# Gate matmuls around the last scale's transpose, the next attention begun in the output stage, and a new order of the attention steps

## The chip, the cores and the metric

The kernel runs on one core of a Trainium2 chip (trn2). Its time is in device microseconds. TensorE multiplies matrices and writes to PSUM; VectorE, ScalarE and GpSimd do the rest (GpSimd does not touch PSUM here); SyncE (SP) issues most DMAs, GpSimd a few.

## The reference

Four batches of 576 tokens go through three blocks. The first is attention with 8 heads of width 64: scores q k^T / 8, plus a decay (the difference of running sums of log f), causal, softmax, times v. The second takes x (the heads side by side, 512 wide):

```
mixed = real(fft(fft(x, axis=1), axis=2))
u = x + mixed
un = (u - mean) / sqrt(var + 1e-6)
x2 = u + relu(un @ w_ch1) @ w_ch2          # 512 -> 2048 -> 512
```

The third is gated over tokens:

```
h = relu(x2 @ w_in); u, v = h[:512], h[512:]
v_n = (v - mean) / sqrt(var + 1e-6)
out = (u * (w_spatial @ v_n + b_spatial)) @ w_out
```

## The kernel before, in words

Values are split into two float16 parts (high and low), and each product is three matmuls (`PASSES`), so most of the time goes to matmuls with 128 x 128 weights.

For one batch the work has two halves. The *attention half* takes four head pairs. Each has a load of q and k into a buffer `a` (`attn_load`), a stack (`attn_stack`: transposes `pk` and `pq`, high and low parts back into `a`, then DMAs `S<-a` into the operands S1 and S2), five max groups (`attn_max`: matmuls `mxd`, `mxa`, `mxb`, `mxc`, reductions on VectorE, and the transposes `mxt` that bring the row maxima into S2), four score groups (`attn_scores`: `sc`, two exponentials, the low part by a subtraction on VectorE, or on GpSimd in batch 0 where `XPOOL` says so) and the product with v (`attn_pv`). v is loaded into `vraw`, reduced and scaled (`v_load`, `v_prep`). Then come `fold` (sums and differences that halve the transform), the token stage `dft1` (tile `yps`), the feature stage `dft2` (tile `eo`, sums added to X) and `norm_tile` (statistics, `un`, and the transposes `tr` into `unT` and `uT`).

The *matmul half* is `mlp1` and `mlp2`. `mlp1` takes three tiles of 192 tokens, for each eight pairs of `first` (`ph`) and `second` (`acc`). At the end of a tile, `acc` is added to `uT` (L927), its largest value `xmx` is reduced (L931), and `scale` turns it into a power of two: a transpose on TensorE (`p2ps`, L268), a short chain on VectorE, and the scaled tokens in `unT` (L938, L939). The scale of the third tile is kept as `state[b]["last"]` and called in `mlp2`. `mlp2` makes the gate half v in five token tiles (`vpart`, tile `pvv`, then its normalisation on ScalarE, VectorE and GpSimd), the u half (`upart`, tile `pu`), the spatial product (`vs`), its split into `gT` and `GT`, and the output (`po`, `ob`, DMA).

The two halves overlap: while TensorE does the matmul half of batch b, the attention half of batch b + 1 is dealt out between its pieces. `mlp1` and `mlp2` are generators that yield a nominal time after each piece (3.87, 2.6, 2.0, 1.7); `xlater` lists the attention steps with nominal times from the table `LATER`, and `run` issues at each yield all steps whose time has come:

```
while evs and (t1 is None or evs[0][0] <= t1):
    evs.pop(0)[1]()
```

So the order on TensorE is written out by hand (`MANUAL`). The lists of the other engines are made by a planner, which places an instruction when its own time model has it ready, by priority in the order of the program. Each engine then works its list in order. SP's list is by hand for batch 0's attention half (`START`), and by the planner after it.

Buffers tie the order too. `a` of one batch and `gu` of the other share one buffer (tag "a"), `vraw` and X share one (tag "X"), and `wps`, `xe`, `xo`, `vr`, `un`, `es`, `tt` and `ob` share three (tag "s2"). PSUM has two pieces for the attention half (`px`) and two of each of two kinds for the matmul half (`py`). Batch 0's attention half runs before the rest, beside the loading and splitting of the weights (`load_w`: GpSimd multiplies by the sign, L363, and subtracts, L366); what is left of the weights and `load_spatial` (transposes `wpps`, L388) is dealt out in batch 0's matmul half by `wsteps`.

Of the kernel before, what the change touches and what calls it, by code (L numbers as in the profile page):

```python
# [15 lines left out]
AF = mybir.ActivationFunctionType  # L16
# [34 lines left out]
QSTART = [0, 128, 256, 320, 448]  # L51
# [74 lines left out]
score1 score1 score1 score1 score1 max2 score1 score1 score1 max2 score1 score1 load3 max2 max2  # L126
max2 score1 w17 part0 score1 pv1 max2 pv1 max2 stack3 stack3 max2 w33 max2 max2 w32 score2
score2 score2 w3 score2 score2 score2 max3 score2 max3 score2 score2 max3 max3 score2 score2
max3 max3 score2 max3 max3 max3 max3 pv2 score3 score3 score3 score3 score3 score3 score3 score3
pv2 w0 w1 score3 score3 part1 score3 score3 part2 w2 pv3 w1 pv3 part3 fold0 fold0 fold2 fold1  # L130
fold1 w1 fold2 tok0 tok1 tok1 tok0 w1 w0 feat0 feat0 w0 w0 feat1 feat0 norm0 feat1 w0 feat2
feat1 w1 norm0 norm0 w2 w2 w3 norm1 norm1 w2 w3 norm0 w2 w4 w4 w4 w3 w3 w4 w5 w4 w5 feat2 w5 w5
w6 norm1 w6 w6 w8 w6 w7 w6 w5 w9 w8 w10 w8 w8 w8 w7 w7 w10 w7 w7 w10 w9 w10 w10 w12 w12 w12 w9
w9 w12 w12 w9 w11 w11 feat2 w11 w14 w14 w13 w11 w11 w13 w15 w13 w13 w13 w15 w14 w15 norm1 w15
w15 w14 w14
"""
# [3 lines left out]
def tile_kernel(  # L140
# [40 lines left out]
    o = 0  # L181
# [325 lines left out]
    def attn_max(b, hp):  # L507
# [459 lines left out]
    def mlp2(b):  # L967
# [27 lines left out]

        def vpart(i):
            n = 128 if i < 4 else 64
            rowscale(i)
            pv = yps("pvv", [128, DM])
            for kc in range(4):  # L1000
                for j, (a, e) in enumerate(PASSES):
                    T.matmul(  # L1002
                        pv[:n, :], xT[:, a, kc, 128 * i:128 * i + n], WI[:, e, kc, DM:2 * DM],
                        start=(kc == 0 and j == 0), stop=(kc == 3 and j == 2),
                    )
            vr = rp.tile([128, DM], F32, name="vr", tag="s2", bufs=NS2)
            A.activation(out=vr[:n, :], in_=pv[:n, :], func=AF.Relu)
# [108 lines left out]

    def xlater(b):

# [8 lines left out]

        L = LATER
# [114 lines left out]
```

## Time and profile before

| | us |
|---|---|
| median of 3 runs | 1000.13 (997.85 to 1002.47) |
| profiled execution | 997.69 |
| its span, first to last instruction | 995.9 |
| TensorE busy | 855.9 (86%) |
| VectorE / ScalarE / GpSimd busy | 596.6 / 397.9 / 270.5 |
| mean granted TensorE clock | 0.929 |

In the rows, PE is TensorE, PEld its weight loads, DVE VectorE, ACT ScalarE, POOL GpSimd and SP SyncE; SPq is SyncE's list of DMA issues. L512 is a line of the kernel. `mxd<-S` names the tile written and the one read. A bracket such as [7.23 <-DMA S<-a] is the time that the engine stood idle just before, and what ended that.

### The profile page before, as it was taken

To read this page: it belongs to the slowest core of one execution; us is meant where nothing else is said; L and a number is where in the kernel's file an instruction comes from. 1 tells how busy PE (TensorE), PEld (TensorE's weight loads), DVE (VectorE), ACT (ScalarE), POOL (GpSimd) and SP (SyncE) were. 2 spreads that over 40 slices of the span, in tenths; PEclk is the share of its full clock that TensorE was granted. 3 is DMA by queue.
4 is the path that set the end of the run, shared out by engine and by line. 5 is a ranking of instruction groups with operands and counts; after the bars stand their busy time and mean duration, and the time that the engine had idled before them with its cause. 6 is when DMAs were issued, how large, how long until landed. Compare 5 with 4: busy or idle time off the path is not lost.

```text
span 995.9 us, 22491 instructions
## 1 busy us (share of the span) xinstructions
PE 855.9 (86%) x9437; PEld 735.2 (74%) x9437; DVE 596.6 (60%) x1437; ACT 397.9 (40%) x697; POOL 270.5 (27%) x371
## 2 busy tenths in 40 slices
PE   3766335888999799699999799799999799999998
PEld 2655224787899568489999587589999486999884
DVE  4666789796754757365774775465674873122341
ACT  1846455767534333252334234144233334111132
POOL 4565887655500533000000440000000540000010
PEclk9886656898999899899999999899999999999999
DMA  7773316916210000722010001622100001000001
GB/s 152 211 213 100 115 64 195 218 48 171 86 35 18 13 7 2 173 61 48 17 38 2 1 2 49 137 61 62 33 7 2 1 2 43 2 2 1 2 1 53
DMA packets 75020, 60.89 MB, mean 61 GB/s; under 512 B 59869, under 2 KB 60263, under 8 KB 74791
## 3 DMA queue, kind: packets, MB, share of 16 engines
q1 hardware_dynamic: 74199, 58.13, 22.5%
q8 instruction: 74, 1.21, 0.5%
q0 software_dynamic: 720, 1.33, 0.5%
q14 instruction: 27, 0.22, 0.1%
HBM read 40.43 MB, written 4.83 MB: 45 GB/s over the span
## 4 chain that ended last, share of the span: by engine, by line
PE 55%; DVE 4%; DMA 2%; ACT 1%; SPq 0%; issue 0%; POOL 0%; ACTq 0%; DVEq 0%
PE ph L897 14%; PE acc L918 13%; PE vs L1051 6%; PE pu L989 4%; PE po L1069 4%; PE pvv L1002 4%; PE sc L618 1%; PE sc L622 1%; PE pv L685 1%; PE mxt L589 1%; PE tr L868 1%; PE yps L777 1%; DMA S<-a 1%; PE pv L687 1%; PE pv L686 1%; DMA vraw<-in_v_dram 1%
## 5 line engine op out<-in xcount | busy, mean ns | idle before, releaser
L897 PE MATMUL ph<-unT,W 128*128 128x192 f16 x2304 | 216.1, 253 | 4.9 <-DVE unT L712 3.6
L897 PEld LDWEIGHTS <-W 128*128 128x128 f16 x2304 | 199.8, 101 | 10.6 <-issue 4.2
L918 PE MATMUL acc<-hT,W 128*128 128x192 f16 x2304 | 205.7, 246 | 0.0
L918 PEld LDWEIGHTS <-W 128*128 128x128 f16 x2304 | 192.1, 98 | 0.2
L903 ACT ACTIVATE hT<-ph 128x384 f16<-128x384 f32 x96 | 46.9, 489 | 158.9 <-PE ph L897 157.1
L904 DVE SCALAR_TENSOR_TENSOR hT<-ph,hT 128x384 f16<-128x384 f32 x96 | 53.0, 552 | 84.7 <-ACT hT L903 84.7
L642 ACT ACTIVATE P<-sc 128x1024 f16<-128x1024 f32 (+1 forms) x64 | 53.9, 842 | 70.5 <-DVE sc L635 52.9
L656 DVE TENSOR_TENSOR P<-sc,P 128x1024 f16<-128x1024 f32 (+3 forms) x51 | 50.7, 994 | 31.8 <-ACT sc L654 30.7
L618 PE MATMUL sc<-S 128*128 128x256 f16 (+2 forms) x288 | 53.6, 248 | 11.4 <-DVE P L656 5.5
L687 PE MATMUL pv<-vh,P 128*128 128x65 f16 (+2 forms) x480 | 57.6, 200 | 4.6 <-DVE P L656 3.3
L975 POOL COPY tsc<-sc 128x2 f32<-128x2 f32 (+1 forms) x24 | 4.2, 195 | 209.9 <-DVE sc L947 209.5
L495 POOL COPY a<-a 128x2 f16<-128x2 f16 x32 | 5.8, 190 | 197.2 <-ACT a L492 143.9
L685 PE MATMUL pv<-vh,P 128*128 128x65 f16 (+2 forms) x480 | 58.4, 202 | 0.4 <-ACT sc L654 0.4
L1002 PE MATMUL pvv<-WI,unT 128*128 128x512 f16 (+1 forms) x240 | 58.5, 399 | 0.0
L686 PE MATMUL pv<-vh,P 128*128 128x64 f16 (+2 forms) x480 | 57.7, 200 | 0.0
L1051 PE MATMUL vs<-WP,vn 128*128 128x288 f16 x448 | 56.2, 286 | 0.0
L622 PE MATMUL sc<-S 128*128 128x256 f16 (+2 forms) x288 | 54.9, 248 | 0.0
L687 PEld LDWEIGHTS <-P 128*128 128x128 f16 (+2 forms) x480 | 48.7, 108 | 5.2 <-DVE P L656 3.6
L1051 PEld LDWEIGHTS <-vn 128*128 128x128 f16 x448 | 43.7, 98 | 10.9
L685 PEld LDWEIGHTS <-P 128*128 128x128 f16 (+2 forms) x480 | 48.0, 106 | 3.8 <-ACT sc L654 0.6
L363 POOL TENSOR_TENSOR WO<-WO,W 128x512 f32<-128x512 f32 x32 | 42.0, 1319 | 28.9 <-DVE WO L354 24.7
L989 PE MATMUL pu<-unT,WI 128*128 128x192 f16 x576 | 49.3, 246 | 0.0
(229 smaller groups left out, 1675.3 us busy)
## 6 DMA issues: line engine op xcount, KB each, us to landing
S<-a SPq DMA_DIRECT2D x96, 144.2 KB, 2.9
WI<-in_moe_w_ch_dram SPq DMA_DIRECT2D x16, 512.0 KB, 4.3
W<-in_moe_w_ch_dram SPq DMA_DIRECT2D x16, 512.0 KB, 4.3
a<-in_k_dram SPq DMA_DIRECT2D x32, 144.0 KB, 2.8
a<-in_q_dram SPq DMA_DIRECT2D x32, 144.0 KB, 4.7
vraw<-in_v_dram SPq DMA_DIRECT2D x16, 256.0 KB, 4.8
WP<-in_moe_w_in_dram SPq DMA_DIRECT2D x8, 512.0 KB, 4.3
out_dram<-ob SPq DMA_DIRECT2D x16, 256.0 KB, 2.2
```

Of the source, the lines that this page charges most:

```text
L618: T.matmul(ps[:, j, c0:c0 + w], S2[s][:, j, QN + 128 * kt:QN + 128 + 128 * kt], qh, start=i == 0, stop=False,)
L622: T.matmul(ps[:, j, c0:c0 + w], S1[s][:, j, 128 * kt:128 * kt + 128], q1, start=False, stop=last and b not in PEMASK,)
L642: A.activation(out=pt[:, 0], in_=src, func=AF.Exp, scale=1.0 / 2048.0)
L685: T.matmul(ps[:n, j, o0:o0 + 65], hi, vh[:kk, 0, kt, h, :], start=(i == 0), stop=False)
L686: T.matmul(ps[:n, j, o0:o0 + 64], hi, vh[:kk, 1, kt, h, 0:64], start=False, stop=False)
L687: T.matmul(ps[:n, j, o0:o0 + 65], lo, vh[:kk, 0, kt, h, :], start=False, stop=(i == len(jobs) - 1),)
L897: T.matmul(ph[:, c, :], W1[:, a, kc, 128 * ff:128 * ff + 128], unT[:, e, kc, tok(t)], start=(c == 0 and kc == 0 and i == 0), stop=(c == 1 ...
L904: V.scalar_tensor_tensor(out=hT[:, 1], in0=ph, scalar=0.0, in1=hT[:, 0], op0=ALU.max, op1=ALU.subtract)
L918: T.matmul(acc[t][d // 2][:, d % 2, :], W2[:, a, ff, 128 * d:128 * d + 128], hT[:, e, c, :], start=(ff == 0 and i == 0 and d % 2 == 0), st ...
L989: T.matmul(ph[:, c, :], WI[:, a, kc, 128 * ff:128 * ff + 128], xT[:, e, kc, tok], start=(c == 0 and kc == 0 and i == 0), stop=(c == 1 and ...
L1002: T.matmul(pv[:n, :], xT[:, a, kc, 128 * i:128 * i + n], WI[:, e, kc, DM:2 * DM], start=(kc == 0 and j == 0), stop=(kc == 3 and j == 2),)
L1051: T.matmul(ps, vn[:kk, a, s, 128 * c:128 * c + 128], WP[:kk, e, s, tok], start=i == 0, stop=i == len(jobs) - 1,)
```

## The change

- The gate stage: `vpart` is divided into `vmat` (matmuls) and `vnorm` (scale factors and normalisation). Two groups of gate matmuls now come before the transpose of the last scale, and the first normalisation, a u group, the second normalisation and the third gate group after it. Before, one gate group with its normalisation came first.
- Attention steps of batch b + 2 are put in the list before the matmul half of b begins instead of after it, so those with negative times are issued within the output stage of b. Times change in `LATER`, batch 1 has a table of its own (`SECOND`), and `V1` goes.
- `attn_max` no longer transposes column 576, a second copy of token 288 (one value a head), by a matmul of its own; VectorE copies it from column 288.
- `VSIGN`: the sign of weight tiles 0, 1 and 5 is put in by VectorE and not by ScalarE and a GpSimd multiplication. `XADDV`: in batch 0, the feature sums of token tile 0 are added on GpSimd. `XPOOL`: in batch 0, the low part of the second score group of the last head pair is made on GpSimd.
- `START` is broken into other lines; its words are the same.

```
-VSIGN = range(0, 0)
-LATER = {'per': 20.875, 'off': -10.0, 'v': (-8.0, 7.0, 9.5), 'load': (17.0, 20.0), 'max': (7.5, 9.5, 12.0, 16.0, 18.5), 'score': (24.5, 23.5, 26.5, 35.5), 'pv': 38.5, 'fold': (93.5, 94.61, 97.7), 'tok': (109.0, 112.27), 'feat': (113.5, 117.99, 119.21), 'norm': (127.0, 121.0, 122.5, 133.5, 126.0), 'out': (134.53, 135.55, 139.09, 142.58, 134.16)}
+VSIGN = (0, 1, 5)
+LATER = {'per': 21.047, 'off': -10.01, 'first': -10.02, 'v': (-8.38, 6.04, 10.17), 'load': (27.96, 17.77), 'max': (7.48, 9.42, 11.98, 15.89, 18.19), 'score': (24.13, 23.07, 26.13, 35.18), 'pv': 38.84, 'fold': (92.29, 93.4, 97.55), 'tok': (109.1, 115.66), 'feat': (118.95, 120.08, 120.91), 'norm': (130.1, 121.74, 128.73, 133.36, 129.96), 'out': (134.19, 138.29, 138.61, 142.1, 132.79)}
+MLP = [26 * 3.87 + 5 * 2.6 + 6 * 2.0 + 8 * 1.7 + n * 2.6 for n in (4, 5)]
-NORM2 = (0.1, 2.673, 2.948)
-V1 = (14.0, 15.5, 16.5)
+NORM2 = (0, 2.838, 3.101)
+SECOND = {'per': 20.875, 'off': -10.13, 'first': -9.5, 'v': (4.87, 15.39, 16.25), 'load': (18.8, 21.49), 'max': (7.5, 9.5, 12.0, 15.56, 18.5), 'score': (24.5, 22.76, 26.5, 35.5), 'pv': 38.16, 'fold': (97.35, 97.43, 100.52), 'tok': (104.42, 111.18), 'feat': (112.33, 117.99, 116.42), 'norm': (128.81, 125.43, 119.33, 134.84, 127.84), 'out': (135.15, 135.63, 139.17, 142.25, 134.24)}
-XADDV = (0, 4)
+XADDV = (4,)
-XPOOL = (3, 3, 4, 3)
+XPOOL = (3, 4, 4, 3)
...
-            jobs = [(t, QSTART[t], 0, QWIDE[t]) for t in range(5)] + [(2, S, 32, 1)]
-            for t, o, r, n in jobs:
+            for t, o in enumerate(QSTART):
+                n = QWIDE[t]
                 T.matmul(
-                    pm[96:128, j, o:o + n], mc[r:r + n, j, t, :], eyeh[r:r + n, r:r + n],
+                    pm[96:128, j, o:o + n], mc[:n, j, t, :], eyeh[:n, :n],
...
-        A.activation(out=S2[s][96:128, :, 0:S + 1], in_=pm[96:128, :, 0:S + 1], func=AF.Copy)
+        A.activation(out=S2[s][96:128, :, 0:S], in_=pm[96:128, :, 0:S], func=AF.Copy)
+        V.tensor_copy(S2[s][96:128, :, S:S + 1], pm[96:128, :, 288:289])
...
-        vpart(0)
+        vmat(0)
+        yield 2.6
+        vmat(1)
         yield 2.6
         state[b]["last"]()
-        vpart(1)
-        yield 2.6
-        vpart(2)
-        yield 2.6
+        vnorm(0)
         upart(0, 0)
         yield 2.0
-        vpart(3)
+        vnorm(1)
+        vmat(2)
+        vnorm(2)
         yield 2.6
-        vpart(4)
+        vmat(3)
+        vnorm(3)
+        yield 2.6
+        vmat(4)
+        vnorm(4)
         yield 2.6
...
-        at("v", *(L["v"] if b > 1 else V1))
+        at("v", *L["v"])
         for hp in range(NP):
-            t0 = L["off"] + L["per"] * hp
-            at(f"load{hp}", t0 - (L["load"][0] if hp == 0 else L["load"][1]))
+            t0 = L["off"] + L["per"] * hp if hp else L["first"]
+            at(f"load{hp}", max(t0 - L["load"][1], last + 0.1) if hp else t0 - L["load"][0])
+            last = t0
...
-        nxt = xlater(1)
+        nxt = xlater(1, {**LATER, **SECOND})
...
         for b in range(B):
-            base = now
+            total = MLP[b % 2]
+            if b + 2 < B:
+                nxt = nxt + [(t + total, f) for t, f in xlater(b + 2)]
+            now = 0.0
             for i, dt in enumerate(mlp(b)):
...
-                run(nxt, now - base)
-            total = now - base
-            if b + 2 < B:
-                more = [(t + total, f) for t, f in xlater(b + 2)]
-                nxt = sorted(nxt + more, key=lambda e: e[0])
+                run(nxt, now)
```

## Rows read from the trace of the kernel before

**Rows 1.** Busy time by stretch: PE, PEld, DVE, ACT, POOL (instructions), granted clock, DMA share, GB/s.
```profile
100.00:125.00 25.00, 8.55 (x60) 5.44 (x61) 19.04 (x44) 12.39 (x24) 21.89 (x19) 0.64 0.37 108
...
400.00:425.00 25.00, 16.57 (x111) 11.15 (x110) 10.17 (x26) 5.04 (x8) 0.37 (x2) 0.80 0.71 157
...
875.00:900.00 25.00, 25.00 (x305) 24.99 (x304) 7.25 (x17) 3.88 (x7) 0.30 (x2) 1.00 0.01 2
```

**Rows 2.** TensorE's waits, whole span: who waited for what: us in total, times, longest.
```profile
PE mxd L512 <- DMA S<-a: 26.0, 5, 7.4
...
PE eo L810 <- ACT yc L783: 3.9, 2, 3.7
```

**Rows 3.** Timeline of TensorE, boundary of batch 0 and 1: start, busy us, instruction, idle before.
```profile
410.03 0.66 PE L482 MATMUL pq<-cft,a 96*128 96x96 f32 x6
417.91 1.10 PE L512 MATMUL mxd<-S 126*128 126x128 f16 x4 [7.23 <-DMA S<-a]
...
420.87 0.93 PE L512 MATMUL mxb<-S 126*128 126x128 f16 x4 [1.11 <-DVE mcol L527]
421.59 3.52 PE L897 MATMUL ph<-unT,W 128*128 128x192 f16 x24
```

**Rows 4.** Timeline of VectorE in that wait.
```profile
410.26 2.29 DVE L428 TENSOR_REDUCE vmx<-vraw 128x1 f32<-128x2048 f32 x1 [6.35 <-DMA vraw<-in_v_dram]
```

**Rows 5.** TensorE's waits from 630 to 642 us, boundary of batch 1 and 2.
```profile
PE mxd L512 <- DMA S<-a: 5.3, 2, 5.1
PE mxb L512 <- DVE mcol L527: 1.1, 1, 1.1
```

**Rows 6.** Timeline of TensorE, end of the first stage, batch 1, then batch 3.
```profile
564.45 0.45 PE L268 MATMUL p2ps<-cft,xmx 128*128 128x128 f32 x1 [4.98 <-DVE xmx L931]
564.69 6.87 PE L1002 MATMUL pvv<-WI,unT 128*128 128x512 f16 x24
...
941.76 5.34 PE L1002 MATMUL pvv<-WI,unT 128*128 128x512 f16 x24
```

**Rows 7.** Timeline of TensorE and VectorE, end of the first stage of batch 0.
```profile
343.17 0.87 PE L388 MATMUL wpps<-cft,wps 128*128 128x128 f32 x3 [7.12 <-DMA wps<-in_moe_w_spatial_dram]
...
344.50 0.41 DVE L712 TENSOR_TENSOR xoh<-a,xoh 128x256 f16<-128x256 f32 x1
...
371.71 0.43 PE L799 MATMUL eo<-xeh,tab 128*65 128x1 f16 x9 [1.32 <-DVE tt L824]
```

**Rows 8.** The chain that ended last: start, us, what.
```profile
402.54 5.18 PE po L1069 x24
...
460.60 1.33 PE mxt L589 x12
```

**Rows 9.** Timeline of VectorE: the scaled tokens of batch 1's last tile.
```profile
570.79 0.99 DVE L939 SCALAR_TENSOR_TENSOR unT<-uT,sc,unT 128x768 f16<-128x768 f32 x1
```

**Rows 10.** Timeline of SP's DMA issues, both boundaries.
```profile
398.07 1.05 SPq L467 DMA_DIRECT2D a<-in_q_dram  x2
...
402.95 4.49 SPq L419 DMA_DIRECT2D vraw<-in_v_dram  x5
...
632.80 1.13 SPq L500 DMA_DIRECT2D S<-a  x2
```

**Rows 11.** Line 467, 612 to 635 us: the loads of q and k.
```profile
DMA to landing us min/median/max: 2.7/2.8/2.9
```

**Rows 12.** Busy time by stretch, columns as in rows 1.
```profile
556.70:572.00 15.30, 10.32 (x48) 4.68 (x46) 14.11 (x36) 5.10 (x11) 9.13 (x15) 0.89 0.00 0
388.90:392.10 3.20, 2.70 (x27) 2.44 (x26) 2.49 (x8) 1.89 (x5) 0.00 (x0) 1.00 0.00 0
```

**Rows 13.** Timeline of TensorE in batch 0: a wait of 2.18 us and what followed.
```profile
242.43 0.19 PE L618 MATMUL sc<-S 128*128 128x65 f16 x1 [2.18 <-DVE P L656]
...
243.11 3.66 PE L897 MATMUL ph<-unT,W 128*128 128x192 f16 x24
```

**Rows 14.** The page's costliest groups: count, busy us and mean ns, idle before.
```profile
L363 POOL TENSOR_TENSOR WO<-WO,W 128x512 f32<-128x512 f32 x32 | 42.0, 1319 | 28.9 <-DVE WO L354 24.7
```

More of the change, by code (lines that the diff above doesn't have):

```diff
@@ L126 @@
 score1 score1 score1 score1 score1 max2 score1 score1 score1 max2 score1 score1 load3 max2 max2
[L127 to L135, printed above, removed]
+max2 score1 w17 part0 score1 pv1 max2 pv1 max2 stack3 stack3 max2 w33 max2 max2 w32 score2 score2
+score2 w3 score2 score2 score2 max3 score2 max3 score2 score2 max3 max3 score2 score2 max3 max3
+score2 max3 max3 max3 max3 pv2 score3 score3 score3 score3 score3 score3 score3 score3 pv2 w0 w1
+score3 score3 part1 score3 score3 part2 w2 pv3 w1 pv3 part3 fold0 fold0 fold2 fold1 fold1 w1 fold2
+tok0 tok1 tok1 tok0 w1 w0 feat0 feat0 w0 w0 feat1 feat0 norm0 feat1 w0 feat2 feat1 w1 norm0 norm0
+w2 w2 w3 norm1 norm1 w2 w3 norm0 w2 w4 w4 w4 w3 w3 w4 w5 w4 w5 feat2 w5 w5 w6 norm1 w6 w6 w8 w6 w7
+w6 w5 w9 w8 w10 w8 w8 w8 w7 w7 w10 w7 w7 w10 w9 w10 w10 w12 w12 w12 w9 w9 w12 w12 w9 w11 w11 feat2
+w11 w14 w14 w13 w11 w11 w13 w15 w13 w13 w13 w15 w14 w15 norm1 w15 w15 w14 w14
 """
@@ L994, in upart, with vmat @@
             A.activation(out=gu[:, 2 * fp:2 * fp + 2, tok], in_=ph, func=AF.Relu, scale=2.0 ** -14)
-        def vpart(i):
+        pvs = {}
+        def vmat(i):
             n = 128 if i < 4 else 64
-            rowscale(i)
-            pv = yps("pvv", [128, DM])
+            pvs[i] = pv = yps("pvv", [128, DM])
             for kc in range(4):
@@ L1005, in vpart, with vnorm @@
                     )
+        def vnorm(i):
+            n = 128 if i < 4 else 64
+            pv = pvs.pop(i)
+            rowscale(i)
             vr = rp.tile([128, DM], F32, name="vr", tag="s2", bufs=NS2)
@@ L1115, in xsteps, with xlater @@
         return seqs
-    def xlater(b):
+    def xlater(b, L=LATER):
         seqs = xsteps(b)
@@ L1126, in at @@
                 ev.append((t, lambda: [next(seqs[key]) for _ in range(n)]))
-        L = LATER
-        at("v", *(L["v"] if b > 1 else V1))
+        at("v", *L["v"])
         for hp in range(NP):
-            t0 = L["off"] + L["per"] * hp
-            at(f"load{hp}", t0 - (L["load"][0] if hp == 0 else L["load"][1]))
+            t0 = L["off"] + L["per"] * hp if hp else L["first"]
+            at(f"load{hp}", max(t0 - L["load"][1], last + 0.1) if hp else t0 - L["load"][0])
+            last = t0
             at(f"stack{hp}", (t0, 2))
@@ L1189, in tile_kernel @@
     with tc.manual_schedule(engines=MANUAL):
-        nxt = xlater(1)
+        nxt = xlater(1, {**LATER, **SECOND})
         for i, t in enumerate((4, 3, 2)):
             nxt += [(x + NORM2[0] + NORM2[1] * i, lambda t=t: [next(left[f"norm{t}"]) for _ in range(2)]) for x in (0, NORM2[2])]
-        now = 0.0
         for b in range(B):
-            base = now
+            total = MLP[b % 2]
+            if b + 2 < B:
+                nxt = nxt + [(t + total, f) for t, f in xlater(b + 2)]
+            now = 0.0
             for i, dt in enumerate(mlp(b)):
@@ L1199, in tile_kernel @@
                 now += dt
-                run(nxt, now - base)
-            total = now - base
-            if b + 2 < B:
-                more = [(t + total, f) for t, f in xlater(b + 2)]
-                nxt = sorted(nxt + more, key=lambda e: e[0])
+                run(nxt, now)
+            assert abs(total - now) < 1e-6
             nxt = [(t - total, f) for t, f in nxt]
```

## The prediction

> **What bounds the kernel now.** I read the busy time of each engine by stretch first. Up to about 275 us TensorE waits: 8.55 of 25 us busy between 100 and 125, while VectorE has 19.04 and GpSimd 21.89. Later it is full (25.00 of 25 between 875 and 900), save a few stretches such as 400 to 425 with 16.57 [rows 1]. So after 275 us only what TensorE waits for counts, and its list of waits names it: the max matmuls wait for `S<-a`, 26.0 us in five places [rows 2]. The timeline then shows each place, and whether the granted clock falls from 2.4 to 1.2 GHz behind it.
>
> Boundary of batch 0 and 1: TensorE stands 7.23 us for `S<-a`, then 1.11 us for VectorE, and the next 24 `ph` matmuls take 3.52 us instead of 2.14 [rows 3]. They lose 1.38; the three max groups before them (1.10 and 0.93 the first and last) lose in the same proportion some 1.2. Together 8.34 + 2.6 = 10.9 us. VectorE sat behind the 2.29 us `vraw` reduction in that wait [rows 4]. Boundary of 1 and 2: 5.3 + 1.1 of wait and by the same account 2.5 of clock, 8.9 us [rows 5]. Ends of the first stage in batches 1 and 2: 4.98 us for `xmx`, then 6.87 us for 24 `pvv` matmuls that take 5.34 in batch 3: 6.5 us, twice [rows 6]. End of batch 0: 7.12 us for a `wps` load, and 1.32 for `tt` [rows 7].
>
> **The change, part by part.** Each event is issued at the first yield at or after its time, so I laid the old and new times on the yields. Most come out at the same place. What moves on TensorE: the stack of batches 2 and 3 goes ahead by a whole step, behind `po0` and behind `po1`; two max groups go to the end of the output stage; the `last` transpose goes behind the second gate group; in batch 0 the token stage goes ahead of it, and the folds go behind the last accumulation; features and norms come a step or two later.
>
> *Max transposes.* Two of 12 go, in 16 steps. Twelve take 1.33 us on the chain [rows 8], 0.11 each. All on the path would give 3.5 us; the four of batch 0's attention lie among other waits; below zero is excluded, as nothing is added on TensorE. I take 2.5 us. The new VectorE copy, two columns, has a step of `ph` and `acc` before the scores need it; without that cover it would cost its own length, far below the 0.99 us of a 768-column operation [rows 9].
>
> *Boundary 0 to 1.* `po0` ends at about 396.4 + 2.59 (24 `po` take 5.18) [rows 8], so 399.0; then the stack's transposes ask for `a`. Its loads can't start earlier than now: they wait for the buffer that `gu` holds, which the last split frees. The last two issues stand at 398.07 to 399.12 [rows 10]; such a load lands 2.8 us after its issue [rows 11]. The last one, issued at 398.6, lands at 401.4; the transposes of `pq` (0.6 [rows 3]) then end at 402.0 instead of 400.1: a new wait of 1.9 us, ends 0 and 4.3 (if the loads took that much longer). Behind it on TensorE stand `po1` to `po3` and the last norm transposes, and behind those the output evictions, which have room. From the stack's last matmul, `pq`, to `S<-a` now takes 7.2 us here [rows 3] and 5.1 to 5.3 at the next [rows 5]; `po1` to `po3` and the norm transposes (eight, a third of those in [rows 12]) last 3 x 2.59 + 0.9 = 8.7. So that wait is covered. The queue it passes is SP's: the `vraw` loads hold it for 4.49 us [rows 10]. Here they need the buffer of the last norm transposes, which come behind the stack, so the `S<-a` issues should be first; I put 0.5, ends 0 and 6. Whether a wait of about 2 us lowers the clock is open: one of 2.18 us was followed by 3.66 us for 24 `ph` [rows 13], where 2.14 is full speed, so 1.5 lost; 1.0 us is taken, ends 0 and 2.5. Gain: 10.9 - 1.9 - 0.5 - 1.0 = 7.5 us.
>
> *Boundary 1 to 2.* The stack follows `po1` and the norm transposes, 3 us later relative to the loads, so it finds them landed. But `vraw` becomes ready together with it, and its 4.49 us of issues come first. The cover is three `po`, 7.8 us, against 5.3 plus some 3 of delay: I put 1.5 us, ends 0 and 5, and 1.0 for the clock. Gain: 8.9 - 2.5 = 6.4 us.
>
> *Ends of batches 1 and 2.* The second gate group adds 2.59 us of work ahead of the transpose, so 4.98 becomes 2.4, provided that `xmx` comes when it does now. VectorE is 14.11 of 15.30 us busy there [rows 12], so it sets that moment, and the fold that is issued a step earlier was ahead of it in the program already. With half of the clock loss (0.8) left: 2 x (6.5 - 3.2) = 6.6 us; ends 0 and 13. Next in line: the fourth gate group needs the scaled tokens, ready 7.3 us after the transpose (564.45 to 571.78) [rows 6, 9]. Ahead of it stand one `pu` group, one gate group and the token stage, 2.0 + 2.6 + 2.5 (by columns) = 7.1, so nothing or little. In batch 3 no token stage stands there, but VectorE is not crowded either. I put nothing for it.
>
> *End of batch 0.* The folds now come behind the request for the next `wps` load, so that load no longer waits for a buffer that the folds took first. But the token stage is reached at 336.05 + 2.6 and two groups of spatial transposes (0.3 each; one at the lower clock shows 0.87), so at 339.2, and its last fold split ends at 344.91: 5.7 us of wait instead of 7.12. The 1.32 us at `tt` goes, as the feature stages are no longer back to back; instead the first one directly follows the token stage, whose eviction cost up to 3.7 us before [rows 2]; I take 1.8. Gain: 8.4 - 7.5 = 0.9 us, ends -4 and 8.
>
> *Start.* Three weight tiles trade a GpSimd multiplication (1319 ns [rows 14]) and a ScalarE sign for one more VectorE operation; one subtraction and one tile's additions move from VectorE to GpSimd. That is about 3.9 us off GpSimd and as much onto it. I take zero, ends -4 and 4.
>
> *The clock beside transposes.* In 388.90 to 392.10, with 24 transposes and half a microsecond of idling, the granted clock stays at 1.00 (2.4 GHz) [rows 12]. The Trainium skill ("TensorE: Matmul & The Clock Gate", Part 4: PE-mode transpose) says that transposes don't count as activity in the way matmuls do. By that the stack's 1.1 us of transposes would lengthen its idling. The trace does not agree so far, and the measurement decides.
>
> *Sum.* 2.5 + 7.5 + 6.4 + 6.6 + 0.9 = 23.9, less 1.0 us for norm transposes that may come late, as they do by 0.5 now [rows 12]: 22.9 us. The profiled execution took 997.69 (span 995.9, 1.8 around it), so 974.8; the median, 1000.13, is 2.4 above it: **977 us**.
>
> **The rivals.**
> *S<-a behind vraw.* If SP gets `vraw` first at both boundaries, it can issue it when the norm transposes end, 402.0 + 2.59 + 0.9 = 405.5, until 410.0; six `S<-a` issues of 0.57 [rows 10] take 3.4, the landing 2.8: 416.2. TensorE is there at 410.7: a wait of 5.5 instead of 0.5. At the second the norm transposes end at 620.4 (631.1 less the stack, one `ph` group and three `po`), so 620.4 + 4.5 + 3.4 + 2.8 = 631.1 against 629.1, or 4.1 of wait with the next pair's loads (2.1) ahead. With full clock losses (3.0 more): 977 + 5.0 + 2.6 + 3.0 = 987.6. For it: `vraw` came before `S<-a` so far [rows 10].
> *The clock falls at every wait left.* If transposes count as idling, both boundaries lose the full 2.5: 977 + 3.0 = 980. The clock row speaks against it.
> *The waits close altogether.* VectorE is rid of the `vraw` reduction and of the crowding; the 13 us of waits and clock that I left at boundaries and ends go: 964. The fullness of VectorE speaks against it.
> *The early part eats it.* The waits up to 275 us are VectorE's and GpSimd's; if added GpSimd work lies on the chain to the first norms (its additions stand ahead of a pow there), that costs the 4 us of its bound; with the boundaries as in the first rival and the end of batch 0 at its worst: 987.6 + 4 + 4.9 = 996.5.
> *Slower: the waits are only split.* If VectorE and DMA alone set all these moments, moving TensorE's work cuts each wait in two and removes none. The 33.1 us of waits stay, five places get a second stretch of half clock (2 x 2.5 + 3 x 1.5 = 9.5), the early feature stage adds 1.8, the max transposes give 2.5: +8.8, so 1009. It decides where `S<-a` lands over 8 us behind the stack and `xmx` comes 2.6 us later than now. For it: VectorE 92% busy at the ends. Against it: DMA idles in the output stage until the last split.
>
> **How the numbers follow.** Forecast 0.54 (968 to 985), `S<-a` behind `vraw` 0.15, the clock 0.05, all closed 0.08, early part 0.10, slower 0.08. A change under 0.5% (5 us) can't be told from none here. Faster: 0.54 + 0.15 + 0.05 + 0.08 = 0.82; same 0.10; slower 0.08. The range takes the forecast, the clock, the first rival and most of the closed case: 964 to 991.
>
> **What would show it.** In the new profile: `S<-a` gone from the top of TensorE's waits, a wait of about 2 us at `pk` or `pq` in batch 1's boundary alone, `p2ps` waiting 2 to 3 us instead of 5.0 in two places, granted clock 1.00 across both boundaries or one short fall, `yps` waiting some 6 us near 340, ten transposes a step. I am wrong if `p2ps` still waits 5 us, if `mxd` waits over 3 us behind the output stage, if the fourth gate group waits, or if the first `ph` matmuls come more than 4 us earlier or later than now.

## The result, and the profile after

The changed kernel takes 966.93 us, the median of 4 runs (964.13 to 967.99), against 999.09 of the kernel before in the same comparison (4 runs, 997.85 to 1002.47): ratio 0.967, 95% interval 0.964 to 0.970. The forecast was 977.0. The profiled execution took 966.72 us (span 965.0, mean granted clock 0.941 against 0.929), 31.0 less than that of before; TensorE is busy 844.5 us instead of 855.9.

I cut both spans at the same events on TensorE, and put beside each stretch what the prediction had booked for it (the 2.5 us of the max transposes spread over the three stretches where the next attention runs):

| stretch on TensorE | before, us | after, us | gain | booked |
|---|---|---|---|---|
| start to the first `ph` | 150.2 | 144.7 | 5.5 | 0 |
| to the last `acc` of batch 0 | 183.1 | 179.4 | 3.6 | 0.8 |
| to the last `vs` of batch 0 | 62.4 | 57.1 | 5.3 | 0.9 |
| to the last `acc` of batch 1 (first boundary) | 161.3 | 157.4 | 3.9 | 8.3 |
| to the last `vs` of batch 1 | 56.5 | 52.2 | 4.3 | 3.3 |
| to the last `acc` of batch 2 (second boundary) | 161.9 | 158.6 | 3.3 | 7.2 |
| to the last `vs` of batch 2 | 56.6 | 50.6 | 6.0 | 3.3 |
| to the end | 164.0 | 165.0 | -1.0 | 0 |

Of the 30.9 us, 19.6 are idle time of TensorE, 6.6 are clock, and 4.8 are work at full clock. The total is near the forecast because the boundaries gave half of what was booked while the first 380 us gave 14 where 2 were booked. The 1.0 us that the sum took off for late norm transposes has no stretch of its own and is not in the table. The -1.0 of the last row is work: the eight norm transposes of one token tile now come behind the last `vs` (22 `tr` in that stretch instead of 14), and as many have moved out of the stretch to the last `vs` of batch 1 into the next.

Busy time by stretch, columns as in [rows 1], its three stretches at the same places of the work:

```profile
100.00:125.00 25.00, 9.94 (x70) 6.20 (x71) 19.64 (x44) 12.93 (x24) 19.65 (x17) 0.60 0.43 115
385.00:410.00 25.00, 19.58 (x164) 14.38 (x164) 12.51 (x33) 6.58 (x11) 0.37 (x2) 1.00 0.71 163
...
860.00:885.00 25.00, 25.00 (x306) 25.00 (x304) 5.33 (x9) 2.94 (x6) 0.00 (x0) 1.00 0.01 2
```

The early part is as sparse as before; the boundary has 19.58 us of TensorE in 25 where it had 16.57, at full clock.

The list of TensorE's waits over the whole span (who waited for what: us in total, times, longest), to be laid beside [rows 2]:

```profile
PE mxd L512 <- DMA S<-a: 16.6, 4, 7.0
PE mxt L589 <- DVE mc L583: 13.8, 5, 4.7
...
PE p2ps L268 <- DVE xmx L932: 4.6, 2, 2.3
...
PE ph L898 <- DVE hT L905: 2.7, 2, 2.3
```

`S<-a` is down from 26.0 us, but still first. Of the 16.6 us, 13.8 lie before 275 us, where 13.5 stood; at the boundaries 2.8 of 12.5 are left. `ph` now waits for `hT`. The timeline of TensorE at the first boundary answers to [rows 3] (start, busy us, instruction, idle before):

```profile
387.10 0.69 PE L482 MATMUL pk<-cft,a 96*128 96x96 f32 x6 [2.44 <-DMA a<-in_k_dram]
...
397.02 0.49 PE L512 MATMUL mxd<-S 126*128 126x128 f16 x4
...
404.93 2.14 PE L898 MATMUL ph<-unT,W 128*128 128x192 f16 x24 [2.31 <-DVE hT L905]
406.91 2.14 PE L919 MATMUL acc<-hT,W 128*128 128x192 f16 x24
410.76 1.09 PE L589 MATMUL mxt<-eyeh,mc 128*32 128x128 f16 x10 [1.71 <-DVE mc L583]
```

The stack waits 2.44 us for its loads (1.9 booked), `mxd` waits for nothing (0.5 booked), but two waits for VectorE have come, 2.31 and 1.71 us. The last row also shows ten transposes in 1.09 us where twelve took 1.33 [rows 8]. VectorE's timeline at that moment shows what stood in front (compare [rows 4]):

```profile
402.12 2.29 DVE L428 TENSOR_REDUCE vmx<-vraw 128x1 f32<-128x2048 f32 x1 [1.62 <-DMA vraw<-in_v_dram]
404.33 0.55 DVE L905 SCALAR_TENSOR_TENSOR hT<-ph,hT 128x384 f16<-128x384 f32 x1
```

It is the same reduction of `vraw`, and VectorE stood idle 1.62 us ahead of it, for its loads, with `hT` behind both in its list. Before, it lay inside TensorE's 7.23 us wait and cost nothing. Now TensorE is at its third `ph` group and wants `hT`.

The second boundary on TensorE (compare [rows 5]), then on SP's queue (compare [rows 10]):

```profile
600.74 0.71 PE L482 MATMUL pq<-cft,a 96*128 96x96 f32 x6 [1.59 <-DVE a L493]
...
611.97 0.87 PE L512 MATMUL mxd<-S 126*128 126x128 f16 x4 [2.75 <-DMA S<-a]
...
613.38 3.02 PE L898 MATMUL ph<-unT,W 128*128 128x192 f16 x24
```

```profile
599.06 4.40 SPq L419 DMA_DIRECT2D vraw<-in_v_dram  x5
603.57 1.91 SPq L467 DMA_DIRECT2D a<-in_k_dram  x2
605.58 1.42 SPq L500 DMA_DIRECT2D S<-a  x2
```

The data for `S<-a` were ready at 603.2 (GpSimd's last copy into `a` runs from 602.99), and the queue was at the loads until 605.5. The `ph` behind the wait takes 3.02 us instead of 2.14.

The ends of the first stage, batches 1 and 2 (compare [rows 6]):

```profile
546.09 0.32 PE L268 MATMUL p2ps<-cft,xmx 128*128 128x128 f32 x1 [2.31 <-DVE xmx L932]
546.25 3.43 PE L990 MATMUL pu<-unT,WI 128*128 128x192 f16 x24
...
756.91 0.32 PE L268 MATMUL p2ps<-cft,xmx 128*128 128x128 f32 x1 [2.31 <-DVE xmx L932]
757.07 2.14 PE L990 MATMUL pu<-unT,WI 128*128 128x192 f16 x24
```

Both wait 2.31 us (2.4 booked). The clock fell behind the first (3.43 against 2.14 us for 24 `pu`) and not behind the second.

The end of batch 0 (compare [rows 7]):

```profile
328.29 0.55 PE L388 MATMUL wpps<-cft,wps 128*128 128x128 f32 x3 [1.36 <-DVE WP L395]
...
332.54 0.41 PE L388 MATMUL wpps<-cft,wps 128*128 128x128 f32 x2 [1.11 <-DMA wps<-in_moe_w_spatial_dram]
333.58 1.66 PE L778 MATMUL yps<-tab,xeh 128*128 128x321 f16 x9 [0.64 <-DVE WP L395]
...
335.81 1.18 PE L778 MATMUL yps<-tab,xoh 128*128 128x321 f16 x6 [0.16 <-ACT xoh L712]
```

Where 7.12 us stood there are now 1.36 and 1.11, and the token stage waits 0.64 + 0.16 instead of the 5.7 booked, though the last fold split ended, at 336.21, no earlier after the last `acc` (12.1 us) than before (11.7).

### The profile page after: what moved, and what is told of

It is laid out like the page before. It is cut to its first block, busy times and chain, and to the rows that moved or that the text cites. A ratio compares the mean times of both kernels' runs of the same rounds, so it can differ in the third digit from the quotient of the medians.

```text
span 965.0 us, 22425 instructions
## 1 busy us (share of the span) xinstructions
PE 844.5 (88%) x9405; PEld 730.0 (76%) x9405; DVE 595.8 (62%) x1452; ACT 395.5 (41%) x694; POOL 267.0 (28%) x372
## 3 DMA queue, kind: packets, MB, share of 16 engines
q0 software_dynamic: 720, 1.33, 0.6%
## 4 chain that ended last, share of the span: by engine, by line
PE 58%; DVE 5%; DMA 2%; SPq 1%; issue 1%; ACT 1%; POOL 0%; ACTq 0%; DVEq 0%
PE ph L898 15%; PE acc L919 14%; PE vs L1063 6%; PE pu L990 5%; PE pvv L1004 4%; PE po L1081 3%; PE yps L778 1%; PE sc L619 1%; PE sc L623 1%; PE pv L686 1%; PE tr L869 1%; PE mxt L589 1%; PE pv L688 1%; PE pv L687 1%; DMA S<-a 1%; PE eo L811 1%
## 5 line engine op out<-in xcount | busy, mean ns | idle before, releaser
L898 PE MATMUL ph<-unT,W 128*128 128x192 f16 x2304 | 212.2, 250 | 5.1 <-DVE hT L905 2.7
L688 PE MATMUL pv<-vh,P 128*128 128x65 f16 (+2 forms) x480 | 59.3, 203 | 6.2 <-POOL P L653 6.2
L686 PE MATMUL pv<-vh,P 128*128 128x65 f16 (+2 forms) x480 | 60.0, 205 | 2.9 <-DVE P L657 2.9
L1063 PE MATMUL vs<-WP,vn 128*128 128x288 f16 x448 | 56.5, 286 | 0.0
L688 PEld LDWEIGHTS <-P 128*128 128x128 f16 (+2 forms) x480 | 50.0, 110 | 6.7 <-POOL P L653 6.6
L1004 PE MATMUL pvv<-WI,unT 128*128 128x512 f16 (+1 forms) x240 | 54.7, 381 | 0.0
L687 PEld LDWEIGHTS <-P 128*128 128x128 f16 (+2 forms) x480 | 49.8, 110 | 3.5 <-issue 3.2
L686 PEld LDWEIGHTS <-P 128*128 128x128 f16 (+2 forms) x480 | 49.2, 108 | 3.6 <-issue 0.2
L990 PE MATMUL pu<-unT,WI 128*128 128x192 f16 x576 | 51.5, 250 | 0.0
```

The lines of the kernel that those rows point to most:

```text
L686: T.matmul(ps[:n, j, o0:o0 + 65], hi, vh[:kk, 0, kt, h, :], start=(i == 0), stop=False)
L687: T.matmul(ps[:n, j, o0:o0 + 64], hi, vh[:kk, 1, kt, h, 0:64], start=False, stop=False)
L688: T.matmul(ps[:n, j, o0:o0 + 65], lo, vh[:kk, 0, kt, h, :], start=False, stop=(i == len(jobs) - 1),)
L898: T.matmul(ph[:, c, :], W1[:, a, kc, 128 * ff:128 * ff + 128], unT[:, e, kc, tok(t)], start=(c == 0 and kc == 0 and i == 0), stop=(c == 1 ...
L990: T.matmul(ph[:, c, :], WI[:, a, kc, 128 * ff:128 * ff + 128], xT[:, e, kc, tok], start=(c == 0 and kc == 0 and i == 0), stop=(c == 1 and ...
L1004: T.matmul(pv[:n, :], xT[:, a, kc, 128 * i:128 * i + n], WI[:, e, kc, DM:2 * DM], start=(kc == 0 and j == 0), stop=(kc == 3 and j == 2),)
```

## The experiments

All ratios are to the kernel before, with five rounds for each experiment. Two kernels that are both compared with it differ by the difference of their ratios, with some 4 us of uncertainty (0.003 and 0.002 together). The planner draws the lists of all engines but TensorE anew for each kernel, so an edit can also move things elsewhere; that is why each reading below rests on the stretch in the trace too.

| kernel | ratio | 95% interval |
|---|---|---|
| changed kernel | 0.967 | 0.964 to 0.970 |
| `b_start`, start alone | 0.993 | 0.990 to 0.996 |
| `b_gate`, gate stage alone | 0.993 | 0.991 to 0.996 |
| `b_mxt`, max transposes alone | 0.993 | 0.991 to 0.996 |
| `b_tables`, tables and early steps alone | 0.986 | 0.983 to 0.989 |
| `a_late`, no early steps | 0.972 | 0.970 to 0.974 |
| `a_novmax`, short reduction of v | 0.962 | 0.959 to 0.964 |
| `a_vlate`, v of batch 3 later | 0.966 | 0.964 to 0.969 |
| `a_tail`, old end of batch 0 | 0.970 | 0.967 to 0.973 |
| `a_start`, old start | 0.974 | 0.972 to 0.975 |
| `a_spool`, S<-a by GpSimd | 0.968 | 0.966 to 0.971 |
| `a_spvs`, and the reduction in four | 0.965 | 0.962 to 0.967 |
| `a_best`, GpSimd for batch 3 alone | 0.964 | 0.963 to 0.966 |

### The four parts, each alone

`b_start` has `VSIGN`, `XADDV` and `XPOOL` of the change, `b_gate` its `vmat`/`vnorm` order, `b_mxt` its `attn_max`, each in the kernel before; `b_tables` is the changed kernel with these three put back:

```
b_start:   +VSIGN = (0, 1, 5)   +XADDV = (4,)   +XPOOL = (3, 4, 4, 3)
b_gate:    -vpart(i) ...        +vmat(i), vnorm(i) in the new order
b_mxt:     -jobs = [...] + [(2, S, 32, 1)]   +V.tensor_copy(S2[..., S:S + 1], pm[..., 288:289])
b_tables:  LATER, SECOND, NORM2, MLP and the listing ahead of mlp(b), alone
```

> The kernel before with the three edits of the start alone (signs of tiles 0, 1 and 5 on VectorE, feature sums of tile 0 on GpSimd, one more low part on GpSimd). The prediction's sum: 0, ends -4 and 4, so no change against before and the first ph at about 150. My theory now, from the two traces (first ph 150.17 before, 144.67 after): these three are all that differs before that point but for the max transposes of batch 0, so 5 us less, first ph at about 145, and most of it between the token stage and the norm transposes of batch 0. Rival: the part of the 5.5 us comes from the fewer max transposes and from the steps dealt in later, then this kernel gains under 2 us.

> The kernel before with the new gate stage alone (two groups of gate matmuls ahead of the transpose of the last scale). The prediction: p2ps waits 2.4 instead of 4.98 us in batches 1 and 2, clock loss halved, 3.3 us each, 6.6 us in all, batch 0 near 0. By the trace of after (idle and clock loss in the gate stages of 1 and 2 fell by 3.1 and 4.9): 6 to 9 us. Rival (the waits are only split): xmx comes later by what TensorE does more, p2ps still waits 4 to 5 us, gain under 1.5 us.

> The kernel before with ten instead of twelve max transposes a step, and the copy of two columns on VectorE, alone. The prediction: 2.5 us less (12 of batches 1 to 3 on the path at 0.22 each make 2.6), ends 0 and 3.5. Rival 1: the added VectorE copy stands ahead of something that TensorE waits for, no gain. Rival 2: TensorE's busy time at full clock fell by 4.8 us between before and after, and if all of it comes from these transposes the gain is 4 to 5.

> The changed kernel with the gate stage, the max transposes and the start put back as before: the new tables and the early listing alone. The prediction: both boundaries (7.5 + 6.4) and the end of batch 0 (0.9), less 1.0: 13.8 us under before. By the trace of after, where the two boundary intervals gain 3.9 and 3.3 with the transposes in them and the end of batch 0 gains 5.3: 9 to 12 us, with 2.3 us of wait for hT at the first boundary and 2.7 us for S<-a at the second. If boundaries and gate stage need each other, the four parts add up to clearly less or more than the 32 us of the whole.

Gains: 7.1 us (4.5 to 9.6), 6.6 (4.0 to 9.3), 6.8 (4.4 to 9.1) and 14.3 (11.5 to 17.1). They add up to 34.8; the whole gave 33.1 (29.9 to 36.4). So within some 6 us, the uncertainty of such a sum, the parts do not need each other. Place by place they do act on each other, as `b_tables` shows at the second boundary.

*Gate.* The wait was right. TensorE's waits of `b_gate` from 540 to 800 us hold `p2ps` twice with 2.3, against 4.98 each before:

```profile
PE p2ps L268 <- DVE xmx L931: 4.6, 2, 2.3
```

The two gate stages take 2.64 and 2.63 us less each, which is the wait alone. The clock fell behind both waits as before: 24 `pu` took 3.71 and 2.99 us there, where 2.14 is full speed. The 1.6 us booked for it are not in these stretches, so that 6.6 meets 6.6 is in part luck. The rival of split waits fails: `xmx` came when it had come before.

*Tables.* 14.3 against 13.8 booked (and 9 to 12 expected), but not by the booked route: in its trace the first boundary's stretch gains 2.5 and the second's 5.5 (the `S<-a` wait there is 0.8, the expected 2.7 did not come; the `hT` wait did, 2.7), the end of batch 0 gains 3.6, the two gate stages 1.4 each, and the part up to the last `acc` of batch 0 loses 4.9 in that one execution. At the second boundary SP's queue has the same order as in the changed kernel, but the next pair's loads take 1.11 us to issue instead of 1.91, and `mxd` waits 0.8 us at full clock where the changed kernel waits 2.75 and loses 1.6.

*Max transposes.* TensorE's work at full clock fell by 3.9 us, by 16 steps of 0.24. That is more than the 2.5 booked, and the measured 4.4 to 9.1 lies above both. The rest I can't place: the profiled execution of `b_mxt` (998.56) was the slowest of its seven and shows no other gain.

*Start.* The gain is there, but my place for it was wrong: the first `ph` came at 149.89, not at 145, and the last `acc` of batch 0 at 329.71 instead of 333.25.

### The start undone

`a_start` is the changed kernel with the old `VSIGN`, `XADDV` and `XPOOL`.

> The changed kernel with the three edits of the start put back (signs of tiles 0, 1 and 5 on ScalarE and GpSimd, feature sums of tile 0 on VectorE, one low part on VectorE). The prediction: no difference from the changed kernel, ends -4 and 4. By the kernel with these edits alone, 0.993 [0.990, 0.996] of before: 4.5 to 9.6 us slower than the changed kernel (0.972 to 0.977 of before), the first ph at 148 to 152 instead of 145. Rival: tables and gate stage have since taken the same slack, then under 2 us.

6.6 us slower than the changed kernel; both measurements of the start agree. The waits up to 160 us show where: the changed kernel waits 5.6 us for GpSimd's low part, 2.6 more for the token stage, and less at the feature sums and at the first `ph`. TensorE's waits of `a_start` from 85 to 160 us, then of the changed kernel from 82 to 160:

```profile
PE ph L898 <- DVE unT L713: 3.5, 1, 3.5
...
PE eo L811 <- ACT yc L784: 2.9, 2, 2.2
```

```profile
PE pv L688 <- POOL P L653: 5.6, 1, 5.6
...
PE ph L898 <- DVE unT L713: 1.7, 1, 1.7
...
PE eo L811 <- ACT yc L784: 0.3, 1, 0.3
```

The first `ph` is no safe mark: in the eight profiles with the new start and the new tables it comes between 144.7 and 149.3. The last `acc` of batch 0 is: 323.9 to 327.4 in those eight, 331.2 in `a_start`, 332.8 to 333.3 in the three kernels with the old start and old tables, 338.2 in `b_tables`. Which of the three edits carries it was not tried.

### The end of batch 0 undone

`a_tail` gives batch 1 the old times for folds, token stage, features and norms.

> The changed kernel with the old times for batch 1's folds, token stage, feature stage and norms (fold to out of the table SECOND as in the old table). The prediction booked 0.9 us for what this undoes. By the traces the end of batch 0 (last accumulation to last spatial matmul) takes 57.1 instead of 62.4 us: 4 to 6 us slower than the changed kernel (0.971 to 0.973 of before), with wpps waiting 5 to 7 us again for a load that the folds' buffers hold. Rival: the new gate order covers that wait by itself, under 2 us.

3.1 us slower by the ratios, where 4 to 6 were expected; that alone would not decide. The stretch does: 63.2 us instead of 57.1, with the old waits back, on TensorE's timeline:

```profile
333.77 0.87 PE L388 MATMUL wpps<-cft,wps 128*128 128x128 f32 x3 [7.04 <-DVE xeh L713]
```

and 1.49 us at the token stage and 1.32 at `tt` behind it. The new gate order was in this kernel and did not cover them. So the new times closed that wait. They were all put back together; that it is the folds' times which count is argued from the buffers and not shown alone.

### The early steps undone

`a_late` lists batch b + 2 after the matmul half of b again:

```
-            nxt = nxt + [(t + total, f) for t, f in xlater(b + 2)]    # ahead of the loop over mlp(b)
+            nxt = nxt + [(t + total, f) for t, f in xlater(b + 2)]    # behind it
```

> The changed kernel with the steps of batch b + 2 put in the list after the matmul half of b again, so that no attention step is issued in the output stage; tables, gate stage, transposes and start as changed. The prediction: both boundaries lose what it booked, 7.5 + 6.4 = 13.9 us slower than the changed kernel (0.981 of the time before). By the trace of after, where 8.2 us of wait and clock stay at the first boundary and 6.0 at the second, against 10.9 and 8.9: 5 to 6 us slower (0.972). Rival: the early stack brings nothing, the waits only move; no difference from 0.967.

5.2 us slower, as the trace had it and not as the prediction booked; the two stretches are 159.8 and 161.6 us, 2.4 and 3.0 longer. On TensorE's timeline the old wait is back at both boundaries, 6.39 us at the first and 5.20 at the second, each with 1.1 behind it:

```profile
406.24 0.50 PE L512 MATMUL mxd<-S 126*128 126x128 f16 x2 [6.39 <-DMA S<-a]
```

At the first, the 2.29 us reduction of `vraw` runs from 399.89, inside that wait: hidden again.

### What stands in front of hT

`a_novmax` cuts that reduction, in batches 2 and 3:

```
-in_=raw[:, 0:4, :]
+in_=raw[:, 0:4, :] if b < 2 else raw[:, 0:4, 0:32]
```

> The changed kernel with the reduction of vraw (L428, 2.29 us on VectorE) cut from 2048 to 128 columns in batches 2 and 3; the scale of v there comes from a part of the values only. My theory: the 2.31 us that ph waits for hT and most of the 1.71 us that mxt waits for mc at the first boundary stand behind that reduction; both go, and with them the clock loss of 1.7: 4 to 5.7 us less than the changed kernel (0.961 to 0.963 of before); at the second boundary, where the reduction lies inside the wait for S<-a, nothing. Rival: TensorE has run out of hT for another reason (the max groups' reductions on VectorE), the waits stay, under 1 us.

5.2 us less, and TensorE's timeline at the first boundary has the third `ph` group without a wait, and `mxt` with 0.36 instead of 1.71:

```profile
408.31 2.14 PE L898 MATMUL ph<-unT,W 128*128 128x192 f16 x24
410.29 2.14 PE L919 MATMUL acc<-hT,W 128*128 128x192 f16 x24
412.80 1.09 PE L589 MATMUL mxt<-eyeh,mc 128*32 128x128 f16 x10 [0.36 <-DVE mc L583]
```

The stretch falls from 157.4 to 153.6 us; that of the second boundary stays (158.6, 158.9). The clock gives nothing back: 1.7 us are lost behind `mxt` in the changed kernel and 1.7 behind `pk` here.

The 3.8 us are not the reduction alone. In this kernel the loads had landed when VectorE came to the reduction, so the idling of 1.62 us ahead of it is gone too. `a_vlate` (below), whose edit does not touch this boundary, shows the whole reduction without that idling, on VectorE and on TensorE:

```profile
403.28 2.27 DVE L428 TENSOR_REDUCE vmx<-vraw 128x1 f32<-128x2048 f32 x1
```

```profile
406.07 2.14 PE L898 MATMUL ph<-unT,W 128*128 128x192 f16 x24 [0.60 <-DVE hT L905]
...
411.90 1.09 PE L589 MATMUL mxt<-eyeh,mc 128*32 128x128 f16 x10 [1.71 <-DVE mc L583]
```

The two waits are 0.60 + 1.71 there, 2.31 + 1.71 in the changed kernel, and 0 + 0.36 in `a_novmax`. Where VectorE idles 1.08, 1.62, 2.04 and 3.08 us for the loads (`a_tail`, the changed kernel, `a_start`, `a_spool`), `ph` waits 1.76, 2.31, 2.73 and 3.77, each time 0.7 more. So about 2.0 us are the reduction at the place to which the early stack brought it, and 1.7 are its loads, which land too late for that place. (The stretch of `a_vlate` is no shorter, 158.3 us, as the clock cost 4.9 us in it and not 1.7.)

### What holds S<-a back at the second boundary

`a_vlate` moves the time of batch 3's `vraw` loads from -8.38 to 0.5.

> The changed kernel with the loads of vraw of batch 3 issued at the first step of the matmul half instead of in the output stage. Theory: at the second boundary their 4.40 us on SP's queue stand ahead of S<-a and make the 2.75 us wait of mxd; S<-a is then issued 4 us earlier, the wait and the clock loss of 1.6 go, 2.7 to 4.3 less there; but the reduction of vraw then falls among the first ph and costs up to 2.3 + 1.7 as at the first boundary: between -4.3 and +0.5 us in sum. Rival: the loads of the next pair (1.91 us) or the buffer of the operands hold S<-a, mxd waits 2 us or more as before.

No difference, and no test: the planner put four of the five loads ahead of `S<-a` on SP all the same, and `mxd` waited 3.02 us. `a_spool` takes the `S<-a` of the first head pair off SP instead; `a_spvs` also cuts the reduction in four; `a_best` uses GpSimd for batch 3 alone:

```
+dq = nc.gpsimd if b > 1 and hp == 0 else nc.sync       # a_best: b > 2
-nc.sync.dma_start(S2[s][0:64, ...   -nc.sync.dma_start(S1[s][...
+dq.dma_start(S2[s][0:64, ...        +dq.dma_start(S1[s][...
+for t in range(4): V.tensor_reduce(out=mx[:, 2 + t:3 + t], in_=raw[:, t, :], ...)   # a_spvs, a_best
```

> The changed kernel with the six DMAs S<-a of the first head pair of batches 2 and 3 issued by GpSimd, which has just made the last copies in a, and not by SP. Theory: at the second boundary SP's queue (4.40 us of vraw, 1.91 of the next pair's loads) holds S<-a back from 603.2 to 605.6 and makes the wait of 2.75 us. Issued by GpSimd (0.55 us each, as its wps loads) they end at 606.5 and land by 609.5, where TensorE asks at 609.2: mxd waits 0 to 0.5, clock loss of 1.6 gone, 4 us less. At the first boundary vraw no longer stands behind S<-a, lands some 2.8 us earlier, and its reduction ends before the second hT is wanted: ph waits 0 to 0.5 instead of 2.31, 2 us less. In sum 4 to 8 us under the changed kernel (0.959 to 0.963 of before). Rival: GpSimd's DMAs start or land later by 3 us or more, then mxd waits as long as now or longer at both boundaries, and no gain.

> The same with the reduction of vraw in batches 2 and 3 cut into four of 512 columns, so that hT can come between them on VectorE. Theory (the reduction's length in front of hT and mc is what costs): the wait of mxt for mc, 1.71 us, falls under 1, and none is left at ph: 1 to 2 us less than the kernel with GpSimd's DMAs alone. Rival: the first pieces now stand ahead of the max groups' reductions and wait for their loads, mxb or mxt wait longer, 0 to 2 us more.

> The changed kernel with what paid in each place: the reduction of vraw in batches 2 and 3 cut into four, and GpSimd issuing S<-a of the first head pair for batch 3 alone (for batch 2, where vraw was slowed by it, SP as before). Theory: at the first boundary the 2.31 us at ph go and mxt keeps 1 us, though mxb may wait 1 to 1.5 for the first pieces; at the second the interval up to the last accumulation of batch 2 falls from 158.6 to about 157.0 as in the kernel before this one. 3 to 5 us under the changed kernel, 0.962 to 0.964 of before. Rival: what is taken from one wait comes back in the next (mxb behind the first pieces), no difference from 0.967 that can be measured.

At the second boundary the theory held in part. TensorE's timeline of `a_spool`:

```profile
613.90 0.34 PE L513 MATMUL mxd<-S 126*128 126x128 f16 x2 [1.11 <-DMA S<-a]
...
619.12 0.56 PE L513 MATMUL mxb<-S 126*128 126x128 f16 x4 [1.87 <-DVE mcol L528]
```

1.11 + 0.30 us for `S<-a` instead of 2.75, and no clock loss; but now `mxb` waits 1.87 us for VectorE, where the `vraw` reduction stands ahead of the max groups (613.57 to 615.86, and its last piece until 617.20). The stretch gains 0.7 us, and 1.5 and 1.7 in `a_spvs` and `a_best`.

At the first boundary it failed. SP's timeline and TensorE's, `a_spool`:

```profile
394.88 8.23 SPq L419 DMA_DIRECT2D vraw<-in_v_dram  x5
```

```profile
408.92 3.19 PE L899 MATMUL ph<-unT,W 128*128 128x192 f16 x24 [3.77 <-DVE hT L906]
```

The first `vraw` issue came 5.3 us after `pk` instead of 7.6, as soon as the last norm transposes, which hold its buffer, had ended (394.5). But the five issues took 8.23 us instead of 4.45. `vraw` landed later, and `ph` waited 3.77 us. By the ratios `a_spool` is 1.5 us slower than the changed kernel, no difference that can be told, where 4 to 8 less were expected. Cutting the reduction removed the wait at `ph` and left 1.46 at `mxb` and 1.08 at `mxt` (`a_spvs`). `a_best` is 2.5 us under the changed kernel by the ratios (3 to 5 were expected), less than the two intervals can tell apart; both its boundary stretches are shorter in the trace (156.5 and 156.8 against 157.4 and 158.6), and at the second 0.83 us of the wait for `S<-a` are left and 1.56 at `mxb` have come.

## Why the prediction was right, and where it was not

The direction, the range and the order of size were right: TensorE's waits set the time after 275 us, and the change closes some of them. That the total fell within 10 us of the forecast is in part luck: the two boundaries gave 7.2 us where 15.5 were booked with their transposes, and what they lacked came from the start and the end of batch 0, for which 0.9 were booked. Step by step:

| step | booked | in the traces | experiment |
|---|---|---|---|
| max transposes | 2.5 | 3.9 of work | 6.8 (4.4 to 9.1) |
| boundary 0 to 1 | 7.5 | 3.9, transposes included | both: 5.2 (`a_late`) |
| boundary 1 to 2 | 6.4 | 3.3, transposes included, with eight `tr` more | |
| ends of batches 1 and 2 | 6.6 | 10.3 | 6.6 (4.0 to 9.3) |
| end of batch 0 | 0.9 | 5.3 | 3.1; 6.1 in its stretch |
| start | 0 | 5.5 to the first `ph`; 4 to 7 to the last `acc` of batch 0 (`a_start`) | 7.1 (4.5 to 9.6); 6.6 undone |

*Boundary 0 to 1.* Waits for the loads and for `S<-a` came as booked (2.44 and 0 against 1.9 and 0.5). What failed is the step after them. The prediction had seen that VectorE sat behind the `vraw` reduction in the old wait, and counted the wait as time to be won. It did not ask what that reduction, and the loads that it waits for, would stand in front of once the wait was gone. TensorE then waits 2.31 us at `ph` and 1.71 at `mxt`, which were booked at nothing, and 1.7 of clock are lost where 1.0 was booked. `a_novmax` prices reduction and loads together at 3.8 us of the stretch; beside `a_vlate`, about 2.0 are the reduction.

*Boundary 1 to 2.* The mechanism was named: `vraw`'s issues come ahead of `S<-a`. It was mis-sized: 2.75 us and 1.6 of clock where 1.5 and 1.0 were booked, with the next pair's loads (1.91 us) in the queue too. And `pq` waited 1.59 us for VectorE, a wait for which the sum had no term. In five kernels with the new tables and the new gate stage, the changed one among them, the wait for `S<-a` is 2.75 to 3.60 us; in `b_tables`, with the old gate stage and shorter issues, 0.8. Why the issues take longer in the five was not tried. The first rival was thus right at this boundary and wrong at the other, where SP issued `S<-a` first.

*Ends of batches 1 and 2.* The waits were right to 0.1 us, shown by `b_gate`. The trace has 3.7 us more in these stretches: 2.3 are work that the tables moved out of them (1.1 to 1.2 each, as in `b_tables`), and 1.0 a wait of 0.5 us for the norm transposes that they closed in each. That work comes back in part behind these stretches, as the eight transposes a batch named above. And the 1.0 us taken off for late norm transposes did not come: of three such waits after 275 us one is left.

*End of batch 0.* That the `wps` load is freed from the folds was right. The 5.7 us at the token stage were wrong: I let it start when the last split was done, but its first matmuls read only the first ones, so it began 2.6 us before the last split ended, and found all but 0.16 us of the rest ready.

*Start.* The prediction's own sign of being wrong came here: the first `ph` is 5.5 us earlier, over the 4 it allowed. I weighed 3.9 us off GpSimd against as much onto it and took zero. I did not ask which engine the edits relieve where TensorE waits. Two of the three take work off VectorE, which TensorE waits for at the transposes and the first `ph`; the price, 5.6 us of wait for GpSimd and 2.6 at the token stage, brings that stage only 1.0 us later (112.46 against 111.42 before). That account of the gain is read from the waits; the gain itself is shown.

*The clock.* The prediction asked whether a wait of about 2 us, beside transposes, lowers it. Both happen. Busy time, granted clock, DMA share and rate in 6 us behind such a wait (columns as in [rows 1]): the two `p2ps` of the changed kernel, then behind its 2.44 us at `pk`, and in a fence of its own behind 2.26 us at the same `pk` in `a_best`:

```profile
546.00:552.00 6.00, 5.91 (x35) 4.33 (x36) 5.91 (x26) 3.64 (x8) 2.46 (x8) 0.72 0.00 0
756.80:762.80 6.00, 5.89 (x46) 4.15 (x47) 5.91 (x26) 3.62 (x8) 2.42 (x8) 1.00 0.00 1
387.00:393.00 6.00, 5.84 (x38) 3.74 (x39) 1.77 (x3) 2.59 (x4) 0.37 (x2) 1.00 0.71 158
```

```profile
387.90:393.90 6.00, 5.80 (x27) 3.05 (x28) 1.50 (x2) 1.41 (x3) 0.37 (x2) 0.72 0.78 183
```

The same wait, with the same matmuls around it, cost 1.7 us of clock in one place and nothing in the other. In the ten kernels with the new gate order, ten of the twenty 2.31 us waits at `p2ps` were followed by that loss and ten by none; in the four with the old order all eight waits of 4.98 us were followed by one, of 1.6 to 2.7 us. Booking half of the loss hits no single case, but the mean of these twenty. So the prediction's question about transposes (the Trainium skill, "TensorE: Matmul & The Clock Gate", Part 4: PE-mode transpose) stays open too: the stack's transposes follow that wait in both kernels, and the clock stayed up in one and fell in the other.

## What to carry to other kernels

When a wait is to be closed, list what other engines do under its cover, and see in front of whom that work will stand when the cover is gone: here a 2.29 us reduction and 1.62 us of waiting for its loads, which cost nothing before, took back 3.8 us. For an engine that consumes tiles one by one, ask when the first is ready, not the last. An early part full of waits is not a reason to book zero: ask which engine TensorE waits for at each place and whether the edit takes work off that engine.

## What the runs showed of the hardware

In `a_spool` the issues of SP's queue took longer beside DMAs that GpSimd had issued. With `S<-a` issued ahead of them by SP, five `vraw` issues took 4.45 us; with six `S<-a` issued by GpSimd from 392.3 to 396.0 they took 8.23, from 394.9 on. At the second boundary two issues for `a<-in_q` took 5.36 us, against 0.93 in the changed kernel, where they stand later in the queue. That the other queue is the cause is argued and not shown: the issues of the next pair's loads also differ without it, 1.91 us in the changed kernel and 1.11 in `b_tables`. At the first boundary the six `S<-a` of GpSimd landed 5.3 us after their issue (median), those of SP in the changed kernel 2.7. So there the move off a crowded queue gave back less than the queue had cost (158.3 us for the stretch, against 157.4). The Trainium skill ("Trainium Kernel Development and Optimization", Key Constraints) says that DMAs of all these queues share the same 16 engines and interleave, and that several issuers save only issue time. These rows are in keeping with the first. At this boundary not even issue time was saved: SP's last `vraw` issue ended 13.5 us after `pk` instead of 12.1.
